# A gated scan and an MLP on one NeuronCore: the planner keeps attention groups open on TensorE

## The chip, the cores and the metric

One core of a Trainium2 chip. The metric is the device time of the whole program in microseconds; the median of three runs is given. The engines are TensorE (PE, matmuls; PEld is its weight loads), VectorE (DVE), ScalarE (ACT), GpSimd (POOL) and SyncE (SP), which here only issues DMAs.

## The reference

```python
# q, k, v, a_re, a_im: (4, 8, 768, 48); per batch and head
mag = sqrt(a_re**2 + a_im**2); scale = minimum(mag, 0.999) / (mag + 1e-6)
for t in range(768):
    S = (a_re + 1j*a_im)[t][:, None] * scale[t][:, None] * S   # S is 48 x 48
    S.real += outer(k[t], v[t])
    y[t] = q[t] @ S.real
x = y as (3072, 384)
h = x @ w_in                                   # 384 -> 2048
g = where(h >= 1, h, where(h <= -1, 0, (h + 1)**2 / 4))
out = g @ w_out                                # 2048 -> 384
```

## The kernel before

**Work.** The 4 x 768 tokens are cut into 12 units of 256 tokens of one batch (two chunks of 128 each). Two units make a block of 512 tokens, six blocks in all. For each unit `gates` (line 569) turns the decays into running products and phases on ScalarE and VectorE, multiplies them into keys and queries, and spreads the rows to heads by ten SBUF-to-SBUF DMAs (`spread`, lines 844 to 881). `attend` (line 898) then does, per chunk, on TensorE: scores `sc` (two PSUM banks of four heads), transposes `tp` of the keys, values `yp` (am times V, plus the old state times the queries) and state products `dp`. VectorE masks scores into `am` (line 997) and adds `dp` to the state `st` (line 974); ScalarE copies `tp` to `kT` (line 939) and `yp` to `xr` (line 1050). Six small DMAs per unit move rows inside `xr` (`move`, line 1062), and `split` (line 1114) makes its high and low parts xH and xL. `moe` (line 1145) runs, for 16 slices f of 128 hidden units, nine matmuls of 512 columns into `h` (line 1160), the activation on ScalarE and VectorE, and nine into the three `o` accumulators (line 1235). All weights are decoded on the chip (`weights`, line 410) during the start and block 0. In blocks below SPARE the activation takes two more ScalarE steps (lines 1195 and 1199) in place of one VectorE step (line 1212). In units below ABS_ACT an absolute value is taken on ScalarE (line 794, shown under its helper's line 608), in later ones on VectorE (line 798).

**Order.** Nothing is issued in program order. Every operation is first recorded in a `Plan` with its engine, a modelled cost, its predecessors and sometimes a due time. `order` (line 169) passes due times back to predecessors, then simulates all engines as a list scheduler: at each step the engine that can start soonest takes, of its ready operations, the one due first. `emit` then issues the instructions in the planned order; each engine works its own list in that order and waits where data are late. SyncE (and VectorE, ScalarE) may hold back for a more urgent operation that will be ready soon (lines 232 to 246, QUEUE and HOLD). DMAs are modelled with a latency, and spreads with LATE_MOVE on top. Before the first MoE product `emit` fills planned gaps of TensorE with idle products (lines 277 to 288 and 1283 to 1290).

**Due times around the change.** DUR (line 312) is the modelled length of a block times SLACK, BEGIN its start. MoE pieces (three matmuls) fall due every DUR/16/6. The attention of a unit of block b is due in a window of block b - 1: WINDOW, EARLY for block 1, HEAD for block 0 (lines 908 to 914), and it is cut into five `visit`s (line 1077) spread evenly over the window. The parts of a visit are glued: when one is planned and the next already has all its predecessors planned, that one is forced next (lines 271 to 273). When not, TensorE may take MoE pieces in between.

**PSUM and SBUF places.** Attention tiles rotate through three PSUM banks `at0` to `at2`, so a part may have to wait until VectorE or ScalarE has emptied the bank that it takes. A batch's state rotates through two buffers (line 955). The upper triangular mask and the ones behind it are one tile, `sums` (line 334).

Of the kernel before, what the change touches and what calls it, by code (L numbers as in the profile page):

```python
# [10 lines left out]
F32 = mybir.dt.float32  # L11
# [53 lines left out]
LATE_MOVE = 1000  # L65
TABLE = 1294
FIRST = 81000
SLACK = 1.04
# [4 lines left out]
QUEUE = (2, 0.0)  # L73
WINDOW = (0.0, 0.7)
EARLY = (0.15, 1.05)
HEAD = ((15000, 8000), (8000, 2000))
HOME = 4
SPARE = 2
# [3 lines left out]
ABS_ACT = 5  # L82
# [42 lines left out]
class Plan:  # L125
# [43 lines left out]
    def order(self):  # L169
# [35 lines left out]
        forced = []  # L205
        while done < n:
# [4 lines left out]
            else:  # L211
                best = None
                for e in free:
                    while avail[e] and avail[e][0][1] in taken:
                        heapq.heappop(avail[e])
# [10 lines left out]
                t, e = best  # L226
                while wait[e] and wait[e][0][0] <= t:
# [44 lines left out]
            if nxt is not None and not left[nxt]:  # L272
                forced.append(nxt)
# [48 lines left out]
def gated_scan_moe(  # L322
# [11 lines left out]
    sums = const.tile([P, 2, P], F32, name="sums")  # L334
    mask = sums[:, 0]
    make_upper_triangular(nc, mask)
    nc.gpsimd.memset(sums[:, 1], 1.0)
# [560 lines left out]
    def attend(u):  # L898
# [25 lines left out]
        def transposes(c):  # L924
            cs = slice(c * CH, (c + 1) * CH)
            out = []
            for g in range(2):
# [19 lines left out]
                carry.setdefault("kT", []).append(KT)  # L947
            return out

        def products(c):  # L950
            kT = carry.pop("kT")
            DP = bank([P, NH, D], f"dp_{u}_{c}")
            V_c = carry["V"]
            old = carry.get(b)
            ST = tl(turn_of(f"st{b % 2}", 2), [HR, NH, D], F32, f"st_{u}_{c}")
            carry[b] = ST

            def run():
                for i in range(NH):
                    for a in (0, 64):  # L960
# [4 lines left out]
                            V_c[0].get()[:, V_c[1], i * D : (i + 1) * D],  # L965
# [4 lines left out]
            def tail():  # L970
                if old is None:
                    fn = lambda: V_.tensor_copy(ST.get(), DP.get()[:HR])
                else:
                    fn = lambda: V_.tensor_tensor(ST.get(), old.get(), DP.get()[:HR], op=ALU.add)
                pl.op("DVE", dve(DM), fn, r=[DP] + ([old] if old else []), w=[ST])

            return [(NH * 124, run, [*kT, V_c[0]], DP, tail)]
# [33 lines left out]
        def values(c, ams, st):  # L1011
# [5 lines left out]
            def part(prs):  # L1017
                Y = bank([P, len(prs), CH], f"yp_{u}_{c}_{prs[0]}")

                def run():  # L1020
                    for i, pr in enumerate(prs):
                        for kind in (0, 1):
                            if kind == 0 and st is None:
                                continue
                            for e in range(2):
# [3 lines left out]
                                if kind == 0:  # L1029
# [4 lines left out]
                                        start=True,  # L1034
                                        stop=False,
                                    )
                                else:
# [4 lines left out]
                                        start=st is None,  # L1042
                                        stop=True,
# [46 lines left out]
        if part == 0:  # L1090
            carry.pop("kT", None)
        state_after = lambda c: part * NC + c < S // CH - 1
        for c in range(NC):
# [9 lines left out]
            pending = (ams, carry.get(b))  # L1103
# [476 lines left out]
```

## Time and profile before

| | us |
|---|---|
| median of 3 runs | 578.7 (578.28 to 579.27) |
| the profiled execution, its own time | 577.35 |
| its span | 575.6 |
| TensorE busy | 561.4 (98%) |
| VectorE busy | 434.5 (75%) |
| ScalarE busy | 406.1 (71%) |
| first MoE product starts at | 70.41 |
| last o product ends near | 568.2 |

The span is the profiler's first to last instruction; the execution's own time holds a little more around it. Matmuls are pipelined, so a single one looks longer than what it adds: nine in mid-stream add 2.04 us. The gap of a group of products is therefore read from start to start.

### The profile page before, as it was taken

What the parts mean: (1) busy time and instruction counts of PE and PEld (TensorE: products, weight loads), DVE (VectorE), ACT (ScalarE), POOL (GpSimd) and SP (SyncE); (2) the same over time, 40 slices, a digit from 0 to 9 for tenths busy, and PEclk for the clock granted to TensorE, in tenths of its full rate; (3) what the DMA queues carried; (4) which work ended last, traced back from release to release, by engine and by line L of the source; (5) the groups of instructions that cost most, each with busy time, mean ns of one, the idle gap of its engine ahead of it and who ended that gap; (6) DMA issues with size and microseconds to landing.
All of it is one profiled execution on the core that took longest, in us unless ns stands there. A gap on an engine that the chain in (4) does not pass through costs nothing.

```text
span 575.6 us, 9984 instructions
## 1 busy us (share of the span) xinstructions
PE 561.4 (98%) x3922; PEld 478.4 (83%) x3922; DVE 434.5 (75%) x625; ACT 406.1 (71%) x654; POOL 1.7 (0%) x20
## 2 busy tenths in 40 slices
PE   8999999999999999999999999999999999999995
PEld 7798978888888888888888888888888888888883
DVE  4999999999979498579589878887885544455452
ACT  7776799887998998975576666667643333369972
POOL 1000000000000000000000000000000000000000
PEclk9999999999999999999999999999999999999999
DMA  8676571773641614712601613402312200078811
GB/s 352 250 198 192 163 262 55 192 282 114 188 173 48 195 68 125 237 57 82 174 2 52 202 56 102 153 2 85 114 56 72 74 1 7 21 265 309 298 42 61
DMA packets 23527, 77.42 MB, mean 134 GB/s; under 512 B 4528, under 2 KB 10288, under 8 KB 23472
## 3 DMA queue, kind: packets, MB, share of 16 engines
q1 hardware_dynamic: 23472, 76.70, 40.8%
q8 instruction: 33, 0.54, 0.4%
q14 instruction: 22, 0.18, 0.1%
HBM read 51.90 MB, written 4.72 MB: 98 GB/s over the span
## 4 chain that ended last, share of the span: by engine, by line
PE 78%; DVE 12%; ACT 5%; DMA 2%; issue 1%; SPq 0%; ACTq 0%; DVEq 0%
PE o L1235 30%; PE h L1160 29%; PE sc L989 6%; PE yp L1038 3%; PE yp L1030 3%; PE dp L962 2%; PE tp L933 1%; PE idle L1290 1%; ACT ai L608 1%; DVE kq L725 1%; DMA xr<-xr 1%; DMA ai<-in_art_dram 1%; DVE g L1204 1%; ACT x L608 1%; DVE raw_i L440 1%
## 5 line engine op out<-in xcount | busy, mean ns | idle before, releaser
L1160 PE MATMUL h<-xH,wi 128*128 128x512 f32 x576 | 180.6, 395 | 1.2 <-DVE g L1204 0.9
L1235 PE MATMUL o<-gh,wo 128*128 128x512 f32 x576 | 180.4, 394 | 0.0
L1160 PEld LDWEIGHTS h<-xH,wi 128*128 128x128 f32 x576 | 106.2, 188 | 22.6 <-DVE g L1204 1.1
L1235 PEld LDWEIGHTS o<-gh,wo 128*128 128x128 f32 x576 | 106.3, 188 | 21.6 <-issue 0.7
L1204 DVE TENSOR_TENSOR g<-h,s 128x512 f32<-128x512 f32 x96 | 65.9, 687 | 63.1 <-ACT s L1185 45.6
L1160 PE MATMUL h<-xL,wi 128*128 128x512 f32 x288 | 112.6, 391 | 0.0
L1235 PE MATMUL o<-gl,wo 128*128 128x512 f32 x288 | 112.5, 391 | 0.0
L1185 ACT ACTIVATE s<-h,cst 128x512 f32<-128x512 f32 x96 | 65.7, 685 | 42.0 <-PE h L1160 38.9
L1218 ACT CAST gh<-g 128x512 fp32r<-128x512 f32 x96 | 59.1, 616 | 46.0 <-DVE g L1212 43.6
L1222 DVE TENSOR_TENSOR gl<-g,gh 128x512 fp32r<-128x512 f32 x96 | 66.0, 687 | 31.9 <-ACT gh L1218 31.8
L1160 PEld LDWEIGHTS h<-xL,wi 128*128 128x128 f32 x288 | 54.1, 188 | 12.1 <-DVE xL L1137 0.4
L1235 PEld LDWEIGHTS o<-gl,wo 128*128 128x128 f32 x288 | 54.1, 188 | 11.6
L608 ACT ACTIVATE ai<-ai 128x768 f32<-128x768 f32 x49 | 41.2, 843 | 19.1 <-DVE ai L777 8.6
L989 PE MATMUL sc<-hd 96*128 96x128 f32 x384 | 49.6, 278 | 0.0
L989 PEld LDWEIGHTS sc<-hd 96*128 96x128 f32 x384 | 47.0, 192 | 2.2
L1212 DVE SCALAR_TENSOR_TENSOR g<-s,g 128x512 f32<-128x512 f32 x64 | 44.2, 691 | 1.8
L1038 PE MATMUL yp<-am,V 128*64 128x128 f32 x384 | 35.5, 273 | 0.2 <-DVE am L997 0.2
L997 DVE TENSOR_TENSOR am<-sc,sums 128x512 f32<-128x512 f32 x48 | 32.5, 683 | 3.1 <-PE sc L989 2.8
L1290 PE MATMUL idle<-sums,ident 128*128 128x128 f32 x238 | 31.3, 291 | 1.7 <-POOL sums masks.py:66 1.7
L1030 PE MATMUL yp<-hd,st 96*64 96x128 f32 x320 | 32.1, 278 | 0.3 <-DVE am L997 0.3
L1290 PEld LDWEIGHTS idle<-sums,ident 128*128 128x128 f32 x238 | 30.3, 206 | 2.5 <-POOL sums masks.py:66 1.7
L402 ACT ACT_TABLE_LOAD x21 | 26.9, 1283 | 0.4
(104 smaller groups left out, 651.6 us busy)
## 6 DMA issues: line engine op xcount, KB each, us to landing
chk<-in_wl_dram SPq DMA_DIRECT2D x16, 768.0 KB, 5.2
kq<-in_kq_dram SPq DMA_DIRECT2D x12, 768.0 KB, 4.7
ai<-in_ari_dram SPq DMA_DIRECT2D x10, 768.0 KB, 6.1
hd<-x SPq DMA_DIRECT2D x24, 288.0 KB, 4.1
hd<-kq SPq DMA_DIRECT2D x24, 288.0 KB, 4.9
raw_i<-in_wl_dram SPq DMA_DIRECT2D x8, 768.0 KB, 4.6
raw_o<-in_wl_dram SPq DMA_DIRECT2D x8, 768.0 KB, 5.8
V<-in_v_dram SPq DMA_DIRECT2D x12, 384.0 KB, 3.2
```

Of the source, the lines that this page charges most:

```text
L608: lambda: A_.activation(out(), src(), f, **kw),
L989: PE_.matmul(SC.get()[:, i, :], t[:, 0, cs], t[:, 1, cs], start=True, stop=True)
L1030: PE_.matmul(o_, st.get().rearrange("p h e -> p (h e)")[:, lo : lo + 64], head(h)[:, 1, cs], start=True, stop=False,)
L1038: PE_.matmul(o_, V.get()[:, c, lo : lo + 64], ams[pr // 2].get()[:, 2 * (pr % 2) + e, :], start=st is None, stop=True,)
L1160: PE_.matmul(H.get(), weight["i", f // 2].get()[:, f % 2, part, sl], x.get()[:, j, :], start=j == 0 and n == 0, stop=j == NJ - 1 and n == 2,)
L1185: lambda: A_.activation(SS.get(), H.get(), AF.Relu, bias=c_half, scale=-0.5 if spare else 0.5),
L1204: lambda: V_.tensor_tensor(G.get(), H.get(), SS.get(), op=ALU.max),
L1212: lambda: V_.scalar_tensor_tensor(G.get(), SS.get(), 1.0, G.get(), op0=ALU.min, op1=ALU.mult),
L1218: pl.op("ACT", act(T), lambda: A_.copy(GH.get(), G.get()), r=[G], w=[GH])
L1222: lambda: V_.tensor_tensor(GL.get(), G.get(), GH.get().bitcast(F32), op=ALU.subtract),
L1235: PE_.matmul(PO[m].get(), weight["o", f // 2].get()[:, f % 2, part, sl], g.get(), start=f == 0 and n == 0, stop=f == NF - 1 and n == 2,)
L1290: PE_.matmul(idle["h1"], ident, mask, start=True, stop=True)
```

## The change

The planner gets a `closed` part: when a part is taken whose glued successor exists, TensorE takes nothing but that successor, and idles until it is ready. The state of a batch is one tile that is added to in place. The old state times the queries comes after am times V in the accumulation. In `moe` the o pieces are recorded one step behind the h pieces instead of LAG steps; their due times keep LAG. `mask` is a tile of its own, and `sums` is built a second time in the place of the second am tile. Eight constants of the planner and of the split of work change.

```diff
@@ -62,24 +62,24 @@
 LOADS = "SP"
 LOAD, MOVE = 410.0, 240.0
 LATE = 2000
-LATE_MOVE = 1000
+LATE_MOVE = 300
 TABLE = 1294
 FIRST = 81000
-SLACK = 1.04
+SLACK = 1.0
 LAG = 3
 SPREADS = 0
 SPREAD = ("SP", "ACT")
 HOLD = {'DVE': (2, 2000.0), 'ACT': (2, 2000.0)}
-QUEUE = (2, 0.0)
-WINDOW = (0.0, 0.7)
-EARLY = (0.15, 1.05)
+QUEUE = (1, 20000.0)
+WINDOW = (0.3, 0.7)
+EARLY = (0.15, 0.9)
 HEAD = ((15000, 8000), (8000, 2000))
 HOME = 4
-SPARE = 2
+SPARE = 1
 LEAD = 8000
 WARM = 0.85
 BRIDGE = 4
-ABS_ACT = 5
+ABS_ACT = 3
 LO_PE = 3
 INFLATE = 1.6
 SPLIT_DUE = 3000
@@ -203,6 +203,7 @@
         done = 0
         taken = set()
         forced = []
+        closed = None
         while done < n:
             if forced:
                 i = forced.pop()
@@ -211,6 +212,16 @@
             else:
                 best = None
                 for e in free:
+                    if e == "PE" and closed is not None:
+                        if closed in taken:
+                            closed = None
+                        elif left[closed]:
+                            continue
+                        else:
+                            t = max(free[e], ready[closed])
+                            if best is None or t < best[0]:
+                                best = (t, e)
+                            continue
                     while avail[e] and avail[e][0][1] in taken:
                         heapq.heappop(avail[e])
                     while wait[e] and wait[e][0][1] in taken:
@@ -224,6 +235,10 @@
                     if best is None or t < best[0]:
                         best = (t, e)
                 t, e = best
+                if e == "PE" and closed is not None:
+                    forced.append(closed)
+                    closed = None
+                    continue
                 while wait[e] and wait[e][0][0] <= t:
                     _, i = heapq.heappop(wait[e])
                     if i not in taken:
@@ -269,8 +284,8 @@
                 if not left[s]:
                     enable(s)
             nxt = self.glued.get(i)
-            if nxt is not None and not left[nxt]:
-                forced.append(nxt)
+            if nxt is not None:
+                closed = nxt
         self.start, self.end, self.due = start, end, due
         return sorted(range(n), key=lambda i: (start[i], i))
 
@@ -331,9 +346,10 @@
 
     ident = const.tile([P, P], F32, name="ident")
     make_identity(nc, ident)
-    sums = const.tile([P, 2, P], F32, name="sums")
-    mask = sums[:, 0]
+    mask = const.tile([P, P], F32, name="mask")
     make_upper_triangular(nc, mask)
+    sums = sb.tile([P, 4, CH], F32, tag="am1", name="sums", bufs=1)[:, :2]
+    make_upper_triangular(nc, sums[:, 0])
     nc.gpsimd.memset(sums[:, 1], 1.0)
     consts = [math.log(1e-6), math.pi / 2, 0.5, TINY, T_MIN, 0.0, 1.0, DECAY]
     cst = const.tile([P, len(consts)], F32, name="cst")
@@ -944,16 +960,16 @@
                     )
 
                 out.append((4 * 83, run, [hd[h // 3] for h in GROUPS[g]], TP, tail))
-                carry.setdefault("kT", []).append(KT)
+                carry.setdefault(("kT", c), []).append(KT)
             return out
 
         def products(c):
-            kT = carry.pop("kT")
+            kT = carry.pop(("kT", c))
             DP = bank([P, NH, D], f"dp_{u}_{c}")
-            V_c = carry["V"]
-            old = carry.get(b)
-            ST = tl(turn_of(f"st{b % 2}", 2), [HR, NH, D], F32, f"st_{u}_{c}")
-            carry[b] = ST
+            first = b not in carry
+            if first:
+                carry[b] = tl(f"st{b % 2}", [HR, NH, D], F32, f"st_{b}")
+            ST = carry[b]
 
             def run():
                 for i in range(NH):
@@ -962,19 +978,19 @@
                         PE_.matmul(
                             DP.get()[a : a + 64, i, :],
                             kT[i // 4].get()[:, k : k + 64],
-                            V_c[0].get()[:, V_c[1], i * D : (i + 1) * D],
+                            V.get()[:, c, i * D : (i + 1) * D],
                             start=True,
                             stop=True,
                         )
 
             def tail():
-                if old is None:
+                if first:
                     fn = lambda: V_.tensor_copy(ST.get(), DP.get()[:HR])
                 else:
-                    fn = lambda: V_.tensor_tensor(ST.get(), old.get(), DP.get()[:HR], op=ALU.add)
-                pl.op("DVE", dve(DM), fn, r=[DP] + ([old] if old else []), w=[ST])
-
-            return [(NH * 124, run, [*kT, V_c[0]], DP, tail)]
+                    fn = lambda: V_.tensor_tensor(ST.get(), ST.get(), DP.get()[:HR], op=ALU.add)
+                pl.op("DVE", dve(DM), fn, r=[DP], w=[ST])
+
+            return [(NH * 124, run, [*kT, V], DP, tail)]
 
         def scores(c):
             cs = slice(c * CH, (c + 1) * CH)
@@ -1019,7 +1035,7 @@
 
                 def run():
                     for i, pr in enumerate(prs):
-                        for kind in (0, 1):
+                        for kind in (1, 0):
                             if kind == 0 and st is None:
                                 continue
                             for e in range(2):
@@ -1031,16 +1047,16 @@
                                         o_,
                                         st.get().rearrange("p h e -> p (h e)")[:, lo : lo + 64],
                                         head(h)[:, 1, cs],
-                                        start=True,
-                                        stop=False,
+                                        start=False,
+                                        stop=True,
                                     )
                                 else:
                                     PE_.matmul(
                                         o_,
                                         V.get()[:, c, lo : lo + 64],
                                         ams[pr // 2].get()[:, 2 * (pr % 2) + e, :],
-                                        start=st is None,
-                                        stop=True,
+                                        start=True,
+                                        stop=st is None,
                                     )
 
                 def tail():
@@ -1087,9 +1103,8 @@
 
         todo_visits = []
         pending = None
-        if part == 0:
-            carry.pop("kT", None)
         state_after = lambda c: part * NC + c < S // CH - 1
+        state_of = lambda: carry.get(b)
         for c in range(NC):
             before = [] if pending is None else values(c - 1, *pending) + products(c - 1)
             sc, ams = scores(c)
@@ -1100,8 +1115,7 @@
             else:
                 visit(sc)
                 visit(tp)
-            pending = (ams, carry.get(b))
-            carry["V"] = (V, c)
+            pending = (ams, state_of())
         last = values(NC - 1, *pending)
         if state_after(NC - 1):
             last = last + products(NC - 1)
@@ -1249,11 +1263,11 @@
                     due=t0 + STEP * (f + LAG - 0.5 + m / 6),
                 )
 
-        for k in range(NF + LAG):
+        for k in range(NF + 1):
             if k < NF:
                 gemm1(k)
-            if k >= LAG:
-                gemm2(k - LAG)
+            if k:
+                gemm2(k - 1)
         for m in range(NJ):
             OB = tl(turn_of("s", 3), [P, T], F32, f"ob_{blk}_{m}")
             i = pl.op(
```

## Rows read from the trace of the kernel before

**Rows 1.** the page's busy times, the whole span
```profile
PE 561.4 (98%) x3922; PEld 478.4 (83%) x3922; DVE 434.5 (75%) x625; ACT 406.1 (71%) x654; POOL 1.7 (0%) x20
```

**Rows 2.** stretch, length, busy us of PE, PEld, DVE, ACT, POOL; PEclk, DMA share, GB/s
```profile
41.16:64.75 23.59, 22.39 (x338) 21.25 (x336) 23.45 (x32) 17.50 (x28) 0.00 (x0) 1.00 0.61 190
64.75:70.41 5.66, 5.40 (x50) 5.21 (x47) 5.20 (x9) 2.98 (x6) 0.00 (x0) 1.00 0.50 146
70.41:153.00 82.59, 81.36 (x609) 68.87 (x610) 81.03 (x114) 73.43 (x115) 0.00 (x0) 1.00 0.58 189
153.00:238.00 85.00, 85.00 (x564) 71.63 (x563) 63.30 (x90) 80.33 (x131) 0.00 (x0) 1.00 0.41 125
```

**Rows 3.** the chain that ended last, in order of time: start, us, what
```profile
33.29 8.04 PE idle L1290 x72
...
65.89 4.04 DMA xr<-xr
...
226.13 2.26 PE o L1235 x9
...
230.43 2.04 PE o L1235 x9
```

**Rows 4.** TensorE's timeline, attention of units 3 and 4: start, us, instruction
```profile
138.93 1.05 PE L989 MATMUL sc<-hd 96*128 96x128 f32 x8
...
141.20 0.82 PE L933 MATMUL tp<-ident,hd 96*128 96x96 f32 x8
...
157.78 0.50 PE L933 MATMUL tp<-ident,hd 96*128 96x96 f32 x4
...
164.29 0.49 PE L933 MATMUL tp<-ident,hd 96*128 96x96 f32 x4
```

**Rows 5.** VectorE's timeline at the same places
```profile
140.14 0.54 DVE L974 TENSOR_TENSOR st<-st,dp 96x384 f32<-96x384 f32 x1
140.60 0.68 DVE L997 TENSOR_TENSOR am<-sc,sums 128x512 f32<-128x512 f32 x1
...
159.71 1.29 DVE L997 TENSOR_TENSOR am<-sc,sums 128x512 f32<-128x512 f32 x2
```

**Rows 6.** SyncE's DMA issues, timeline
```profile
34.55 2.01 SPq L392 DMA_DIRECT2D hd<-kq  x3
...
226.16 4.15 SPq L392 DMA_DIRECT2D hd<-x  x5
230.36 3.47 SPq L392 DMA_DIRECT2D hd<-kq  x5
234.04 3.67 SPq L392 DMA_DIRECT2D xr<-xr  x6
```

**Rows 7.** DMA issues by line: KB each, median us to landing
```profile
hd<-kq SPq DMA_DIRECT2D x24, 288.0 KB, 4.9
```

**Rows 8.** groups of instructions by line and shape: busy us, mean ns, idle before
```profile
L608 ACT ACTIVATE ai<-ai 128x768 f32<-128x768 f32 x49 | 41.2, 843 | 19.1 <-DVE ai L777 8.6 <-DMA ai<-in_ari_dram 4.1 <-DVE ai L622 3.4
L1212 DVE SCALAR_TENSOR_TENSOR g<-s,g 128x512 f32<-128x512 f32 x64 | 44.2, 691 | 1.8
...
L1195 ACT ACTIVATE s<-s,cst 128x512 f32<-128x512 f32 x32 | 23.1, 723 | 0.5
...
L1199 ACT ACTIVATE s<-s 128x512 f32<-128x512 f32 x32 | 20.1, 628 | 0.4
...
L798 DVE TENSOR_SCALAR ai<-ai 128x768 uint32<-128x768 uint32 x7 | 3.9, 556 | 1.5 <-ACT ai L608 1.4
```

**Rows 9.** POOL and ScalarE at the start, timeline
```profile
1.36 0.29 POOL masks.py:66 TENSOR_SCALAR_AFFINE_SELECT sums<-sums 128x128 f32<-128x128 f32 x1
...
4.03 0.93 ACT L608 ACTIVATE x<-ai,cst 128x768 f32<-128x768 f32 x1 [1.68 <-DMA ai<-in_art_dram]
```

**Rows 10.** busy us by stretches, the end of the span
```profile
568.20:572.00 3.80, 0.20 (x3) 0.09 (x2) 0.29 (x2) 0.66 (x2) 0.00 (x0) 1.00 0.68 220
572.00:576.00 4.00, 0.00 (x0) 0.00 (x0) 0.00 (x0) 0.00 (x0) 0.00 (x0) 0.69 0.04 10
```

## The prediction

> **What bounds the kernel now.** I read the page's busy shares first, then the busy time by stretches, then the chain that ended last, then TensorE's timeline around attention. TensorE is busy 98% of the span [rows 1]. By stretches [rows 2] it is full, 85.00 of 85.00 us, once block 1 runs, and 81.36 of 82.59 in block 0; ahead of the first MoE product (70.41 us) it works on the attention of units 0 and 1 (22.39 of 23.59 us) and then fills 5.40 of 5.66 us with idle products while the moves of `xr` land (4.04 us in the chain, [rows 3]). The granted clock is 1.00 throughout, 2.4 GHz. VectorE is nearly full too in block 0 (81.03 of 82.59) but has room in block 1 (63.30 of 85), where ScalarE is the fuller one (80.33). So behind 70.41 us a change gains only by taking work or switches off TensorE, ahead of it by starting the first product earlier; and it loses by any stall of TensorE. A switch has a price: nine o products behind an attention visit take 2.26 us in the chain, nine in mid-stream 2.04 [rows 3], so 0.22 us for each return from a visit.
>
> The profiled execution took 577.35 us (575.6 of span and 1.75 around it); the median of the three runs is 578.7, 1.35 higher. I sum against 577.35 and add 1.35 at the end.
>
> **Open groups.** The planner now picks nothing else for TensorE between two glued parts. Each of units 2 to 11 has five visits (lines 1093 to 1108), 50 in all. In TensorE's timeline I find two that MoE products broke: unit 3's (scores at 138.93, transposes at 141.20) and unit 4's (four transposes at 157.78, the other four at 164.29) [rows 4]. Joining them saves 2 x 0.22 = 0.44 us. If TensorE must wait instead: unit 3's transposes needed the state add (0.54 us from 140.14) and the first am of the next chunk (0.68 us from 140.60), so from the end of the scores at 139.98 to 141.28, with the first transposes fitting in, some 1.2 us; unit 4's second half needed the first of the two am's of 159.71, done near 160.4 [rows 5], while the first half ended at 158.28: 2.1 us. Ends: 0 to 3.3 us. I take 0, because unit 4's first visit now falls due 13 us later against MoE (0.15 x 89.2, below), when VectorE's backlog is gone, and unit 3's place moves as well. What queues behind a waiting TensorE is every MoE product, and so h, then ScalarE's s and VectorE's g.
>
> **Due times.** DUR is SLACK x (66,048 + 23,200 ns): 92.8 us becomes 89.2. For units from block 2 on, WINDOW gave each unit 0.35 x 92.8 = 32.5 us for five visits, one per 6.5 us; now 0.2 x 89.2 = 17.8, one per 3.6 us. A piece of three MoE products is due every STEP/6, 0.97 and now 0.93 us, so 6.7 pieces between two visits become 3.8. Where none is left between two, a switch falls away. Ends: none of the 32 gaps of those units, or 15 (3.3 us); I take three, 0.66 us, since the transposes still wait for am and the next visit for kT, which keeps the gaps apart. The last visit of a block was due 20.4 us before the next block's begin (0.78 of DUR) and is now due 17.0 us before it (0.81). Behind it come the copy, six `xr` moves, xH and xL. Their cover is the rest of the block's MoE: in front of block 1 those steps left TensorE 5.66 us without real work [rows 2], and at the second handover the moves were issued only at 234.04, behind ten `hd` spreads of 226.16 [rows 6]. As unit 6's first visit falls due 13 us later, its spreads now rank behind the moves, so I cost the handover at nothing; without that, 7.6 us of spreads return, and 5.7 + 7.6 = 13.3 is still inside 17.0. EARLY ends sooner (0.9 for 1.05): unit 3's last visit is due at 0.875 of block 0 instead of 0.935, 11 us before block 1 instead of 6, which only helps there.
>
> **LATE_MOVE.** The planner believes that the `hd` spreads land 0.7 us sooner. Ahead of unit 0's scores it puts idle products for 0.85 of the planned gap (line 286): the filler of 8.04 us from 33.29 [rows 3] shrinks by 0.6. The chain goes through the filler, not through a transfer, so the data were there before. When? The three `hd` spreads of kq were issued over 2.01 us from 34.55 [rows 6]; the scores of the first group need the first two, the second of them issued near 35.2, and the large kq spreads take 4.9 us to land [rows 7]: 40.1, against the filler's end at 41.33. So there are about 1.2 us to gain at most, and 0 if the second group's heads wait instead. I take 0.6, and that it reaches the first MoE product, since TensorE is the fuller engine in between.
>
> **QUEUE.** SyncE no longer holds itself free for a more urgent transfer unless that one is 20 us more urgent. At worst one spread's issue (0.6 us, a third of 2.01 [rows 6]) gets in front of the first `xr` move; at best 0.2 us of holding goes. I take 0.
>
> **SPARE, ABS_ACT.** Block 1 loses two ScalarE steps in each of 16 f (723 and 628 ns) and gains one on VectorE (691 ns) [rows 8]: 21.6 us off ScalarE, 11.1 us onto VectorE, which goes from 63.3 to 74.4 of 85 us [rows 2]. Both are hidden under a full TensorE. Units 3 and 4 take the absolute value on VectorE: 2 x 0.56 = 1.1 us more, for 2 x 0.84 less on ScalarE [rows 8]. Both lie in block 0, where VectorE's room is 82.59 - 81.03 = 1.56 us: hidden by that alone, and if the cover is gone up to 1.1 us. I take 0.
>
> **The rest at nothing.** The state in place: the same count of adds, and each already follows the products behind the y products that read the old state. am times V first: the same matmuls, and am and state are both older than the visit. Ends: 0.1 us either way. o products built one step behind: their due times keep LAG, so only ties move. The separate mask adds a memset and a select on POOL (0.29 us, [rows 9]) before the constants that ScalarE first needs at 4.03, when it still waits for a DMA [rows 9]. That `sums` sits in the second am's place makes that am wait for the last running sums, which TensorE has behind it when it turns to filler at 33.29 [rows 3], ahead of any scores.
>
> **Sum.** 577.35 - 0.44 - 0.66 - 0.6 = 575.65; with 1.35 the median is 577.0 us, 0.3% less.
>
> **Rivals.** *Nothing that can be told* (0.31): the open rule acts on two visits of 50, the scores end up waiting for their transfer, no gap closes; 578.7 - 0.44 = 578.3. For it: TensorE is full and its products are the same. Against it: the filler lies in the chain.
> *TensorE stalls in open groups* (0.23): at both places it waits as priced, and nothing else comes: 578.7 + 3.3 = 582.0. For it: VectorE is full up to 153 us, and closer visits leave am and state less time; it decides from the point at which the stalls exceed the 1.7 us gained, about one VectorE queue of three operations. Against it: 48 visits ran unbroken.
> *The clock falls in such a wait* (0.03): with TensorE out of work at the end, the granted clock went from 1.00 in 568.2 to 572 to a mean of 0.69 in the next 4 us [rows 10]. If each stall brought as much work again at 1.2 GHz, the 3.3 us would count twice: 585.3. The Trainium skill (TensorE: Matmul & The Clock Gate, HAM oscillation) says that waits between bursts of products put TensorE back to its lower clock, so that the next burst starts cold; by that rule keeping the engine open is worse than breaking a group. The rows agree for an engine left empty; no row has it for a wait as short as 2 us.
>
> **Numbers.** A difference under 0.2% (1.2 us) a measurement of this kernel can't tell from none. Faster 0.43, same 0.31, slower 0.26. The faster case by itself reaches from 573.7 (all gains at their far ends: 0.44 + 3.3 + 1.2) to 577.5. The range joins the stalls: 573.7 to 582.0.
>
> **What would show it.** Right: no MoE product inside a visit; a filler before unit 0's scores of about 7.4 us and the first h near 69.8; fewer than 50 separate visits; `xr` moves ahead of the next `hd` spreads at a handover; block 1's VectorE at 74 us. Wrong: a wait of TensorE for am or st, in block 0 above all; a first h later than 70.4; a wait of h for xH or xL at a block's start.

## The result, and the profile after

The changed kernel takes 579.99 us (median of 20 runs, 577.99 to 582.48) against 578.71 for the kernel before (20 runs, 577.72 to 580.62): a ratio of 1.0023, 95% interval 1.0012 to 1.0033. It is a little slower, by about as much as can be told from nothing. The time lies inside the forecast range, and on the other side of the old time than the forecast of 577.0. The profiled execution took 577.99 us (span 576.2), the fastest of its 20, so its trace shows the loss at its smallest; `after_again` below has a trace of an ordinary execution. (The diff changes seven constants: LATE_MOVE, SLACK, QUEUE, WINDOW, EARLY, SPARE and ABS_ACT. The section on the change says eight.)

The page's busy times and the busy time by stretches of the changed kernel (columns as in [rows 2]), against [rows 1, 2]:

```profile
PE 560.3 (97%) x3916; PEld 476.9 (83%) x3916; DVE 446.0 (77%) x643; ACT 388.8 (67%) x620; POOL 2.0 (0%) x22
```

```profile
41.16:64.75 23.59, 21.78 (x331) 20.64 (x331) 23.49 (x33) 17.48 (x27) 0.00 (x0) 1.00 0.63 196
...
70.41:153.00 82.59, 81.67 (x613) 69.42 (x613) 80.93 (x114) 70.78 (x109) 0.00 (x0) 1.00 0.53 180
153.00:238.00 85.00, 83.93 (x558) 70.39 (x557) 73.58 (x109) 64.07 (x102) 0.00 (x0) 1.00 0.39 122
```

VectorE's busy time rises by 11.5 us and ScalarE's falls by 17.3, most of it in block 1, as asked. What matters stands in TensorE's column: in block 1 it is no longer full (83.93 of 85.00, before 85.00), and in the attention ahead of block 0 it works 21.78 us where it worked 22.39. TensorE's timeline at the start shows the second place, and the first gain of the forecast with it:

```profile
32.82 7.53 PE L1304 MATMUL idle<-mask,ident 128*128 128x128 f32 x66
40.19 2.02 PE L1005 MATMUL sc<-hd 96*128 96x128 f32 x16
42.04 0.49 PE L949 MATMUL tp<-ident,hd 96*128 96x96 f32 x4
43.97 0.55 PE L949 MATMUL tp<-ident,hd 96*128 96x96 f32 x4 [1.43 <-DVE am L1013]
...
69.89 0.74 PE L1174 MATMUL h<-xH,wi 128*128 128x512 f32 x2
```

The filler is 7.53 us, six products fewer than the 72 of before (8.20 us in this view, 8.04 in the chain of [rows 3]), and the first h comes at 69.89, 0.52 earlier. The second transposes wait 1.43 us for the masked scores, which come when VectorE gets to them; before, it was 0.82. So the 0.67 us that the filler lost is nearly all waited for again here. From the first h to the small product behind the last o (fp, at 568.70, before at 568.21) the loop takes 498.81 us against 497.80. So in this pair of traces 0.5 us are won at the start and 1.0 lost behind it. TensorE's listed waits in the loop are 2.0 us where before had 1.2. One of 0.93 at 77 us stands in both; the new one is at the handover from block 0 to block 1. TensorE's row, and the chain of waits there, in order of time (pieces under 0.2 us left out):

```profile
157.47 0.73 PE L1174 MATMUL h<-xH,wi 128*128 128x512 f32 x2 [1.03 <-DVE g L1218]
```

```profile
148.28 5.13 DMA xr<-xr
153.43 0.41 ACT xH L1144
153.96 0.37 issue
154.33 0.39 ACT xH L1144
154.72 0.63 ACT s L1209
155.48 0.50 issue
156.18 0.53 ACT s L1213
156.73 0.70 DVE g L1218
157.47 0.97 PE h L1174 x3
```

TensorE waits 1.03 us there for g. ScalarE works in order: the activation of a slice (s) stands behind casts to xH that wait for a move of `xr`, and the move, 16 KB, takes 5.13 us to land. ScalarE also has a step on the decays of a later unit (line 624, 0.84 us from 155.25) between the last two steps of s. SyncE's queue at this handover and at the next:

```profile
144.44 2.62 SPq L408 DMA_DIRECT2D hd<-x  x4
147.17 0.52 SPq L408 DMA_DIRECT2D ai<-in_ari_dram  x1
147.73 1.14 SPq L408 DMA_DIRECT2D xr<-xr  x2
...
228.65 1.16 SPq L408 DMA_DIRECT2D hd<-x  x2
229.89 3.91 SPq L408 DMA_DIRECT2D xr<-xr  x6
```

Four spreads and a load go out ahead of the first two moves; at the second handover two spreads do, and the other eight follow the moves, as was forecast. The late moves by themselves don't make the wait: in the kernel before, all ten spreads went first and the moves still later, and TensorE did not wait there. Its queue, and TensorE's scores of unit 4:

```profile
151.18 4.71 SPq L392 DMA_DIRECT2D xr<-xr  x6
```

```profile
155.30 1.95 PE L989 MATMUL sc<-hd 96*128 96x128 f32 x16
```

In the changed kernel TensorE has MoE products alone from 145.26 to 164.41: no attention visit lies in the handover that would give ScalarE time. From the second handover on, s waits for the output's transfers, since it takes a buffer that an `out` transfer still reads. The same row of the list of waits of the whole run, of the kernel before and of the changed one (total, times, longest):

```profile
ACT s L1185 <- DMA out_dram<-ob: 1.5, 3, 0.8
```

```profile
ACT s L1199 <- DMA out_dram<-ob: 7.6, 7, 2.3
```

In this trace none of these seven reaches TensorE.

### The profile page after: what moved, and what is told of

Read it like the earlier page. It is cut to its first block, busy times and chain, and to the rows that moved or that the text cites. A ratio compares the mean times of both kernels' runs of the same rounds, so it can differ in the third digit from the quotient of the medians.

```text
span 576.2 us, 9961 instructions
## 1 busy us (share of the span) xinstructions
PE 560.3 (97%) x3916; PEld 476.9 (83%) x3916; DVE 446.0 (77%) x643; ACT 388.8 (67%) x620; POOL 2.0 (0%) x22
## 4 chain that ended last, share of the span: by engine, by line
PE 83%; DVE 6%; DMA 4%; ACT 4%; issue 1%; SPq 1%; ACTq 0%; DVEq 0%
PE o L1249 33%; PE h L1174 32%; PE sc L1005 7%; PE yp L1054 4%; PE yp L1046 3%; PE dp L978 3%; PE tp L949 2%; DMA xr<-xr 2%; DMA out_dram<-ob 1%; ACT ai L624 1%; DMA ai<-in_art_dram 1%; SPq L408 1%; DVE kq L741 1%; DVE x L850 1%; DVE raw_i L456 0%
## 5 line engine op out<-in xcount | busy, mean ns | idle before, releaser
L1226 DVE SCALAR_TENSOR_TENSOR g<-s,g 128x512 f32<-128x512 f32 x80 | 55.2, 690 | 2.3
L624 ACT ACTIVATE ai<-ai 128x768 f32<-128x768 f32 x47 | 39.4, 842 | 13.3 <-DVE ai L793 5.4
L1013 DVE TENSOR_TENSOR am<-sc,mask 128x512 f32<-128x512 f32 x48 | 32.3, 683 | 5.9 <-PE sc L1005 5.8
L1304 PE MATMUL idle<-mask,ident 128*128 128x128 f32 x232 | 29.9, 287 | 1.7 <-POOL mask masks.py:66 1.7
L1304 PEld LDWEIGHTS idle<-mask,ident 128*128 128x128 f32 x232 | 28.9, 202 | 2.5 <-POOL mask masks.py:66 1.7
L1054 PEld LDWEIGHTS yp<-am,V 128*64 128x64 f32 x384 | 22.5, 136 | 7.9 <-issue 4.3
```

The lines of the kernel that those rows point to most:

```text
L624: lambda: A_.activation(out(), src(), f, **kw),
L1054: PE_.matmul(o_, V.get()[:, c, lo : lo + 64], ams[pr // 2].get()[:, 2 * (pr % 2) + e, :], start=True, stop=st is None,)
L1226: lambda: V_.scalar_tensor_tensor(G.get(), SS.get(), 1.0, G.get(), op0=ALU.min, op1=ALU.mult),
L1304: PE_.matmul(idle["h1"], ident, mask, start=True, stop=True)
```

## The experiments

Each version was run 4 to 20 times; a ratio is to the kernel before on the same chip, with its 95% interval. The record also has the mean granted clock of every execution. A stretch at 1.2 GHz lowers it: the trace of `new_constants` below has one such stretch and a mean of 0.994, that of `three_windows_back` two, the second twice as long, and 0.989, and the two traces of the changed kernel have none from 30 us on and means of 0.996 and 0.995.

**The changed kernel again.** 

> The changed kernel unchanged, for a second trace. Its runs spread from 578.0 to 582.5 us, and the trace in hand is the fastest of them. 'Edge' theory (the constants move unit 4's attention out of the end of block 0, so h waits there for VectorE's g, 1.03 us): ratio to before 1.002, and the second trace shows the same wait near 157 us, longer if the run is longer. 'Lead' theory (LATE_MOVE 300 lets unit 0's scores start 0.6 us earlier, so late spreads now stop TensorE): the second trace, if longer, shows the extra wait between 40 and 66 us.

Measured: 1.0017 (1.0001 to 1.0034). Its trace is 2 us longer than the one above, and the loop takes 500.86 us with 3.3 us of waits. The wait of the start is about the same (1.49), the one of the first handover 1.18, and at the second handover the wait of s reaches TensorE, here and once more (0.49 at 258.00):

```profile
250.90 0.69 ACT L1199 ACTIVATE s<-h,cst 128x512 f32<-128x512 f32 x1 [1.54 <-DMA out_dram<-ob]
```

```profile
252.39 0.73 PE L1174 MATMUL h<-xH,wi 128*128 128x512 f32 x2 [0.75 <-DVE g L1218]
```

**Structure or constants.** `old_constants` leaves open groups, state in place, o pieces and the rest as changed and puts all seven constants back; `new_constants` does the reverse, in the kernel before.

```diff
-LATE_MOVE = 300
-SLACK = 1.0
-QUEUE = (1, 20000.0)
-WINDOW = (0.3, 0.7)
-EARLY = (0.15, 0.9)
-SPARE = 1
-ABS_ACT = 3
+LATE_MOVE = 1000
+SLACK = 1.04
+QUEUE = (2, 0.0)
+WINDOW = (0.0, 0.7)
+EARLY = (0.15, 1.05)
+SPARE = 2
+ABS_ACT = 5
```

> The changed kernel with all seven constants back (LATE_MOVE, SLACK, QUEUE, WINDOW, EARLY, SPARE, ABS_ACT); open groups, state in place, am first and the o order stay. 'Edge' and 'lead' both say: back to before or near it, ratio 1.000, but for one stall in unit 3's open visit of 1.0 to 1.3 us (1.002 at most), and a spread of runs like before's. 'Open' theory (the open groups are what costs): ratio 1.002 to 1.004, as the changed kernel or above it.

> The kernel before with the seven new constants alone; groups may be broken, the state has two buffers, the old state's product comes first. 'Edge' and 'lead': as slow as the changed kernel, ratio 1.002, with the wait of h for g near 157 us of 1.0 us and the first h near 69.9. 'Open': back to 1.000 or under it (0.999 by the 0.5 us earlier start).

Measured: `old_constants` 0.9987 (0.9971 to 1.0003), `new_constants` 1.0022 (1.0003 to 1.0041). The loss comes with the constants: on one chip the changed kernel's median is 580.09 us (`after_again`), with the old constants put back 578.60. The structure costs nothing that can be told, and gains nothing either. With the old constants the open rule does wait, at the place that the forecast named (unit 3) and for the operation it named:

```profile
138.71 1.05 PE L1005 MATMUL sc<-hd 96*128 96x128 f32 x8
140.56 1.15 PE L949 MATMUL tp<-ident,hd 96*128 96x96 f32 x8 [0.79 <-DVE st L990]
```

In `new_constants` the wait at the start does more than last. TensorE's timeline, and the busy time of 1 us stretches behind it (last three columns: granted clock, DMA share, GB/s):

```profile
44.24 0.55 PE L933 MATMUL tp<-ident,hd 96*128 96x96 f32 x4 [1.50 <-DVE am L997]
```

```profile
45.00:46.00 1.00, 1.00 (x7) 0.78 (x6) 1.00 (x3) 0.30 (x1) 0.00 (x0) 0.50 0.83 209
46.00:47.00 1.00, 1.00 (x11) 1.00 (x12) 1.00 (x3) 0.00 (x0) 0.00 (x0) 0.50 0.81 152
47.00:48.00 1.00, 1.00 (x16) 1.00 (x14) 0.96 (x3) 0.02 (x1) 0.00 (x0) 0.50 0.34 76
```

The granted clock is 0.50, 1.2 GHz, for three microseconds behind a wait of 1.50; that is some 1.5 us of work lost, and the first h comes at 71.50. Nine other traces with this wait, 1.36 to 1.50 us long, keep 1.00; the changed kernel's two (1.43 and 1.49) are among them. By the recorded clocks the six slowest-clocked of the twelve executions of `new_constants` (0.991 to 0.994) have a median of 581.69 us and the other six (0.995 to 0.998) 579.65, against 579.43 for the kernel before. So its ratio comes in good part from the clock, and that it equals the changed kernel's does not show that the cause is the same.

**The due windows.** `due_times_only` puts the new WINDOW and SLACK alone into the kernel before, `due_times_spare_1` SPARE = 1 as well:

```diff
-SLACK = 1.04
+SLACK = 1.0
-WINDOW = (0.0, 0.7)
+WINDOW = (0.3, 0.7)
```

> The kernel before with WINDOW (0.3, 0.7) and SLACK 1.0 alone. Its start is that of before (first h near 70.4, first wait of unit 0's transposes 0.8 us). 'Edge' theory (attention moved off the block ends is what costs): waits of h for g of 0.5 to 1.5 us near 160 and near 250, none in before, and a ratio of 1.002 to 1.004. Rival 'start' (the longer wait of unit 0's transposes, 1.43 to 1.50 us for 0.82, behind which one trace shows the clock at 1.2 GHz for 3.2 us, is what costs): 1.000.

> The kernel before with WINDOW and SLACK as changed, and SPARE 1. 'ScalarE in the bare stretches': most of the 1.0% that WINDOW and SLACK cost alone is gone, ratio 1.001 to 1.004, no wait of 2 us near 204. If SPARE is no part of it: 1.008 to 1.010 again.

Measured: 1.0098 (1.0077 to 1.0119) and 1.0058 (1.0032 to 1.0083). The windows moved into the old setting cost a whole per cent, and SPARE = 1 gives part of it back. In the first trace the wait that was expected near 160 is not there, the one near 250 is (1.41 us at 256.61). The longest lies in the middle of block 1, at neither handover: ScalarE waits for a load, with s queued behind it; TensorE runs dry and comes back at half its clock:

```profile
199.53 0.85 ACT L608 ACTIVATE ai<-ai 128x768 f32<-128x768 f32 x1 [2.34 <-DMA ai<-in_ari_dram]
```

```profile
204.86 0.72 PE L1160 MATMUL h<-xH,wi 128*128 128x512 f32 x2 [2.17 <-DVE g L1204]
```

```profile
206.00:208.00 2.00, 2.00 (x6) 1.63 (x5) 1.15 (x2) 2.00 (x5) 0.00 (x0) 0.50 1.02 409
208.00:210.00 2.00, 2.00 (x7) 1.56 (x7) 0.69 (x1) 2.00 (x5) 0.00 (x0) 0.71 0.40 164
```

My theory by now was that the windows lose the time on their own account. `late_window` asked whether a window that ends later (0.85, SLACK 1.02, groups breakable, four s buffers) fills the handover again:

```diff
-SLACK = 1.0
+SLACK = 1.02
-WINDOW = (0.3, 0.7)
+WINDOW = (0.3, 0.85)
-            if nxt is not None:
-                closed = nxt
+            if nxt is not None and not left[nxt]:
+                forced.append(nxt)
```

> A version that may beat both, with attention spread further towards the block ends: the changed kernel with breakable groups, four s buffers, WINDOW (0.3, 0.85) and SLACK 1.02. By 'edge', visits nearer to the handover cover it: no wait of h above 0.3 us behind 165, ratio 0.998 to 1.000. If only visits at the start of a block, as before had them, cover the handover: 1.001 to 1.002.

Measured: 1.0100 (1.0078 to 1.0122). The waits did not go (2.00 us at 168.16, 0.76 at 253.52), and at the third handover an `out` transfer holds VectorE's g back, and TensorE for 3.39 us; the clock is 0.50 in 345 to 347:

```profile
342.37 0.69 DVE L1218 TENSOR_TENSOR g<-h,s 128x512 f32<-128x512 f32 x1 [4.99 <-DMA out_dram<-ob]
```

```profile
343.11 0.73 PE L1174 MATMUL h<-xH,wi 128*128 128x512 f32 x2 [3.39 <-DVE g L1218]
```

`windows_back` is the test of the theory: the changed kernel with WINDOW and SLACK alone as before; `three_windows_back` has the old EARLY too.

```diff
-SLACK = 1.0
+SLACK = 1.04
-WINDOW = (0.3, 0.7)
+WINDOW = (0.0, 0.7)
```

> The changed kernel with WINDOW and SLACK alone back at (0.0, 0.7) and 1.04; the other five constants, the open groups and all the rest stay as changed. Theory A, the due windows are what the change lost by, on their own account: with them back the waits at the handovers of blocks go and the ratio falls below the changed kernel's 1.0023, to 0.997 to 1.000. Theory B, the seven constants only work as a set (each other one put back alone made the changed kernel slower): 1.003 to 1.010, slower than the changed kernel, and its waits lie elsewhere.

> As windows_back, and EARLY back at (0.15, 1.05) too, so that all due times are those of the kernel before; LATE_MOVE, QUEUE, SPARE and ABS_ACT stay as changed. Theory A: 0.997 to 1.000, and block 0 to 1 has its visits at the block's end again, as before. Theory B: 1.003 to 1.010.

Measured: 1.0123 (1.0099 to 1.0147) and 1.0140 (1.0118 to 1.0162). The theory fell: with all due times as before, the kernel is slower than with the new ones. In `windows_back` the open group of unit 3 waits 1.59 us for the state, and the clock falls behind it:

```profile
142.46 1.15 PE L949 MATMUL tp<-ident,hd 96*128 96x96 f32 x8 [1.59 <-DVE st L990]
```

```profile
144.00:146.00 2.00, 2.00 (x6) 1.61 (x5) 2.00 (x2) 0.63 (x2) 0.00 (x0) 0.50 0.00 0
```

In `three_windows_back` TensorE has two long waits. The first h waits for xH until 74.20, since the `xr` moves (issued from 65.98 in `windows_back`, 66.02 here) run beside more spreads and land in 4.6 and 5.9 us (medians) where the changed kernel's took 2.7. And the open group of unit 3 waits for the state, behind VectorE's queue:

```profile
74.20 1.22 PE L1174 MATMUL h<-xH,wi 128*128 128x512 f32 x2 [2.96 <-ACT xH L1144]
```

```profile
146.21 1.54 PE L949 MATMUL tp<-ident,hd 96*128 96x96 f32 x8 [2.65 <-DVE st L990]
```

```profile
143.07 1.76 DVE L850 TENSOR_TENSOR kq<-kq,ai 128x1536 f32<-128x1536 f32 x1
144.74 0.96 DVE L476 TENSOR_TENSOR wi<-raw_i,wi 128x768 fp32r<-128x768 f32 x1
145.61 0.55 DVE L990 TENSOR_TENSOR st<-st,dp 96x384 f32<-96x384 f32 x1
```

```profile
146.00:148.00 2.00, 1.79 (x9) 1.73 (x10) 2.00 (x5) 0.69 (x2) 0.00 (x0) 0.50 0.80 295
148.00:150.00 2.00, 2.00 (x6) 1.58 (x5) 2.00 (x3) 0.27 (x1) 0.00 (x0) 0.50 1.03 418
150.00:152.00 2.00, 2.00 (x6) 1.52 (x6) 1.23 (x3) 0.32 (x1) 0.00 (x0) 0.50 0.14 58
```

A kq product and the decoding of weights (wi) lie ahead of the state add in VectorE's list; the group that may not be broken stands still for 2.65 us, and six microseconds at 1.2 GHz follow. That is the rival of stalls in open groups and the clock's rival together, at the predicted place, in a setting in which the change does not run.

The clock is a part of what the slow mixtures lose. All executions of `late_window` (0.988 to 0.993), `windows_back` (0.991 to 0.993) and `three_windows_back` (0.989 to 0.991) have a lower mean than any of the kernel before beside them (0.995 to 0.998). An estimate from these means, with TensorE taken as full: a mean lower by 0.001 costs about 0.58 us. That gives 3.5 of the 6.2 us that `late_window` lost, 2.5 of 7.3 for `windows_back`, 3.9 of 8.4 for `three_windows_back` and 1.8 of 5.0 for `due_times_only`.

**The other constants**, each put back alone into the changed kernel: LATE_MOVE 1000, SPARE 2, QUEUE (2, 0.0), ABS_ACT 5.

```diff
-LATE_MOVE = 300
+LATE_MOVE = 1000
```

> The changed kernel with LATE_MOVE back at 1000 alone. 'Lead': the runs get their narrow spread back and the ratio falls to 1.000; the first h is at 70.4 again. 'Edge': the wait at the end of block 0 stays at 0.5 to 1.5 us, the start is 0.5 us later, ratio 1.002 to 1.004.

```diff
-SPARE = 1
+SPARE = 2
```

> The changed kernel with SPARE back at 2 alone (block 1's activation takes 21.6 us more of ScalarE and 11.1 us less of VectorE). Theory 'ScalarE in the bare stretches' (with attention drawn together, block 1 has 20 us of MoE alone, where three steps of ScalarE per f leave no room for a late load): slower than the changed kernel, ratio 1.003 to 1.006, with a wait of h for g near 200. If SPARE is a step that costs nothing, as the prediction has it: 1.002.

```diff
-QUEUE = (1, 20000.0)
+QUEUE = (2, 0.0)
```

> The changed kernel with QUEUE back at (2, 0.0) alone, so that SyncE holds back for more urgent transfers again. If QUEUE is part of the cost (at the first handover the spreads of unit 4 and a load went out before the moves of xr): the wait of h near 157 shrinks and the ratio falls to 1.000 or 1.001. If it costs nothing, as predicted: 1.002, the wait of 1.0 us stays.

```diff
-ABS_ACT = 3
+ABS_ACT = 5
```

> The changed kernel with ABS_ACT back at 5 alone: units 3 and 4 take the absolute value on ScalarE, 1.1 us off VectorE in block 0, 1.7 us onto ScalarE. If VectorE's 1.1 us is what starves h at the end of block 0: the wait near 157 goes, ratio 1.000 to 1.001. If it is hidden, as predicted: 1.002, the wait stays at about 1 us.

Measured: 1.0028 (1.0012 to 1.0044), 1.0039 (1.0020 to 1.0059), 1.0052 (1.0033 to 1.0072) and 1.0098 (1.0073 to 1.0122). None is below the changed kernel's 1.0023, and ABS_ACT's is clear of its interval; LATE_MOVE's can't be told from it. The wait of h at the first handover is in all four traces (0.65 to 1.52 us, between 158 and 169 us), and the one that was expected near 200 for SPARE in none. So none of the four is shown to be the one that loses; the planner makes another order from each mixture, and no mixture of constants tried is shown to beat either whole set. In the trace of `queue_old` the first h comes at 71.26, 1.4 us later than in the changed kernel's, since it waits 1.23 for xH. In that of `abs_5` the loop takes 500.90 us with 2.7 of waits; its trace is the fastest of its six executions (580.71), and three of the others have clocks of 0.991 to 0.993, so a part of its loss is the clock's. Where the rest goes stays open.

**The start.** `early_scores` gives the kernel before three pairs of idle products fewer ahead of unit 0's scores, LATE_MOVE's effect on the filler alone. `fill_wait` gives the changed kernel six pairs of idle products where the transposes wait.

```diff
+                if u == 0:
+                    extra[len(pl.ops)] = -3
                 visit(sc)
...
+        if i in extra:
+            n += extra[i]
```

```diff
                 visit(tp)
+                if u == 0:
+                    extra[visits[-1][1]] = 6
...
+        if i in extra:
+            n = max(n, 0) + extra[i]
```

> The kernel before with three pairs of idle products (0.67 us) fewer ahead of unit 0's scores; nothing else moves in the plan. The scores start 0.6 us earlier, while am, in VectorE's queue, comes when it came: the wait of unit 0's second transposes grows from 0.82 to about 1.45 us, as in the changed kernel. If 'start' is a cost of its own (the clock falls behind that wait in some executions, 1.6 us each): ratio 1.001 to 1.002 and single runs 1.5 us above the rest. If it costs nothing by itself: 0.999 to 1.000, and all of the changed kernel's loss lies behind the first h.

> The changed kernel with six pairs of idle products (1.34 us) ahead of the second transposes of unit 0, in the wait for am of 1.43 to 1.50 us. 'Start' theory (in some executions that wait drops the clock to 1.2 GHz for about 3 us, 1.6 us each time): the wait shrinks to 0.1 to 0.2 us, no drop, a narrower spread with nothing above 582, ratio 1.000 to 1.001. 'Edge': the same ratio as the changed kernel, 1.002.

Measured: 1.0017 (1.0002 to 1.0033) and 1.0002 (0.9988 to 1.0017). In `early_scores` the scores come 0.6 us sooner, the second transposes wait 1.42 us for am, and the lead is gone at the first h (70.81, before 70.41), which waits for the `xr` moves:

```profile
70.35 0.86 ACT L1133 CAST xH<-xr 128x256 fp32r<-128x256 f32 x2 [2.11 <-DMA xr<-xr]
```

```profile
70.81 0.73 PE L1163 MATMUL h<-xH,wi 128*128 128x512 f32 x2 [0.93 <-ACT xH L1133]
```

Both results lie where the theory 'start' put them, and `fill_wait`'s interval leaves out the 1.002 of 'edge', though its trace keeps both handover waits (0.99 us at 157.60, 0.73 at 252.77). By the clocks, six of the twelve executions of `early_scores` are at 0.993 (median 579.90; the other six 579.28), and none of `fill_wait` is under 0.996 (median 579.16). So in the old setting a part of the cost can be the clock's, though no trace shows where it fell in those six. In the changed kernel it is not: 18 of its 20 executions are at 0.995 or above, and their median is that of all 20. Why `fill_wait` is no slower than the kernel before is therefore open; `fill_wait` is 0.2% below the changed kernel's 1.0023, from another set of runs, and the intervals overlap.

`early_scores` shows one thing more. Its plan behind the first h is that of the kernel before and its listed waits there are as short (1.15 us), yet its loop takes 499.41 us, 1.6 longer. So a difference of 1 us in the loop between single traces can't be put down to the listed waits alone.

**The output's buffers.** `four_s` gives s, g and ob four places instead of three in the changed kernel (three lines, one of them shown); `four_s_fill` adds the idle pairs; `old_constants_s4` takes the old constants, breakable groups and four places; `old_constants_s4_fill` adds three idle pairs to that.

```diff
-            SS = tl(turn_of("s", 3), [P, T], F32, f"s_{blk}_{f}")
+            SS = tl(turn_of("s", 4), [P, T], F32, f"s_{blk}_{f}")
```

> The changed kernel with four buffers for s, g and ob instead of three, in the SBUF that the state's second buffers left. 'Edge' theory, its part at the second handover (s waits for the out transfer that still reads ob in its place, so h waits for g, 1.24 us in three of four traces of the new constants): those waits near 252 and 258 go, the median falls by about 1 us, ratio 1.000; the wait near 157 stays. 'Start': no change, 1.002.

> The changed kernel with both repairs: four s buffers and the six filler pairs in unit 0's wait. If the costs are two separate ones ('start' 0.0015 by fill_wait, 'edge' at the second handover 0.0006 by four_s, of the changed kernel's 1.002), the ratio is 0.9995 to 1.000, a little under either repair alone. If both repaired the same thing, 1.000 to 1.001.

> A version that may beat both: the constants and the breakable groups of before, the changed kernel's state in place, am first and o order, and four buffers for s. 'Edge' says that before has no wait at the block ends to lose, except ScalarE's and VectorE's for the out transfers: ratio 0.998 to 1.000. 'Start' says 1.000.

> A version that should beat both: the constants and breakable groups of before, state in place, four s buffers, and three filler pairs (0.67 us) in unit 0's wait of 0.82 us. 'Start' and 'edge' together: ratio 0.997 to 0.999, the runs close together (none above 579.7); by 'edge' alone as old_constants_s4, 0.9986.

Measured: 1.0011 (0.9995 to 1.0026), 1.0013 (0.9995 to 1.0030), 0.9986 (0.9971 to 1.0001) and 0.9993 (0.9979 to 1.0008). None can be told from the kernel before, and the two repairs don't add up. In the trace of `four_s` the waits near 252 and 258 are gone, as expected, and those of the first handover add up to 1.3 us. No version here is shown to beat both kernels.

## Why the prediction missed the sign

**Open groups: the stalls right, the gain not there.** I took 0 of 0 to 3.3 us for stalls, because later due times move the two places; the loop of the changed kernel has no wait for st or am. That is in part luck: with the same windows, `late_1000` waits 0.53 us for the state at unit 3 and `four_s_fill` 0.33. With old due times put back, in whole or in part, it waits 0.79 us (`old_constants`, I had 1.2 for that place), 1.59 (`windows_back`) and 2.65 (`three_windows_back`), inside the 3.3 for both places. The 0.44 us of saved switches did not come. From start to start, three products behind such a part take 0.78 us for 0.68 in mid-stream, so a return costs 0.10 at these places and not 0.22; in TensorE's two timelines unit 3's scores and transposes with their returns take 1.61 us broken and 1.59 joined, unit 4's 2.53 broken and 2.77 joined.

**Due times: the step that failed.** I took 0.66 us for closed gaps and cost the handover at nothing, because the steps behind the last visit fit in the 17 us before the next block. In place of nothing, the two traces of the changed kernel show new waits of h for g at the handovers: 1.03 us, and 1.18 + 0.75 + 0.49. The time was enough, but time was not what ran short. The old window had visits in the handover itself (scores at 239.79, transposes at 248.43 in the trace before; 249.08 and 252.95 in the one after). Without them TensorE takes MoE slices one after another, each of which needs s, g and gh from in-order engines whose next operation waits for a transfer. I had put a price on xH and xL, and none on s behind a landing `xr` move or behind an `out` transfer. Measured: waits in the loop of 2.0 to 3.3 us against 1.2, and a loop of 498.81 to 500.86 against 497.80. That the constants carry the loss is shown (`old_constants`). That it goes through these waits is not: the trace of `old_constants`, which is no slower than before, has 2.03 us of waits and a loop of 498.88 too, and `fill_wait` keeps the handover waits. That WINDOW and SLACK alone are to blame was my theory and fell with `windows_back`. So the handover's term was wrong at 0, and how much of the 1.28 us between the medians it carries stays open. Few gaps closed: 49 separate attention groups lie behind the first h, before 52. I had counted on five fewer, two by the joins and three by closed gaps; of the three that went, two are the joins, so one gap closed (unit 4's scores and transposes).

**LATE_MOVE: right at its place, wrong at the end.** The filler was forecast at about 7.4 us and is 7.53, the first h at 69.8 and is at 69.89. The second number is luck. The longer wait for am took the filler's gain back, so that the second transposes come 0.30 us earlier than before, and TensorE was already 0.31 us ahead when the filler began (32.82 for 33.13); the rest is `xr` moves that landed sooner. By itself (`early_scores`) the 0.6 us turned into a wait for am, and the first h came later (70.81); in `four_s`, with the same start as the changed kernel, it is at 70.67. I had bounded it by the landing of the spreads at TensorE's side and not asked what VectorE does next.

**QUEUE, SPARE, ABS_ACT: the cover held, the sum's form did not.** Block 1's VectorE was forecast at 74.4 us and is 73.58; most spreads follow the `xr` moves at the second handover; no engine became the bound. At the first handover my bound for QUEUE, one spread's issue of 0.6 us ahead of the moves, was too small: four spreads and a load, 3.1 us of issues, went first. And I costed each constant against the old plan, at 0. Put back singly these three make the ratio 0.0016 to 0.0075 larger; and WINDOW and SLACK cost 0.98% when they enter the old setting and 1.00% when they leave the new one (1.0123 less 1.0023). A sum over parts does not hold in a schedule that is planned anew for each mixture.

**The clock's rival** was given 0.03 for the open groups. The traces have it at three kinds of wait: 1.50 us ahead of transposes, 2.17 and 3.39 ahead of h, 1.59 and 2.65 in an open group, each followed by three to some six microseconds at 1.2 GHz. The Trainium skill (TensorE: Matmul & The Clock Gate, HAM oscillation) says that a wait between bursts of products makes the next burst start cold; these traces agree at those places, and not at the nine waits of 1.36 to 1.50 us that kept the clock. The row for a wait as short as 2 us that the prediction lacked is there now. It is not the cause of the changed kernel's slower median: the clock holds in its two traces, and of its 20 executions only two (0.994 and 0.993) have a mean as low as that of a trace with such a stretch.

**The spread.** I added the old distance of 1.35 us between the profiled execution and the median. For the changed kernel it is 2.0 (577.99 to 579.99), in `after_again` 0.1 (579.96 to 580.09): which execution is profiled is chance, and the distance is no property of a kernel to be added to a sum.

**The signs.** Of what the prediction named for being right, the unbroken visits, the filler, the first h, the fewer groups and block 1's VectorE came out, and the order of the moves in part; of what it named for being wrong, none showed in the loop, though at the start the wait for am grew from 0.82 to 1.43 us. The time went the other way all the same: no sign looked at a wait of h for g.

## What to carry to other kernels

Before a stage handover is cost at nothing, ask what independent work the fullest engine has there while its neighbours wait for transfers; look in the trace at what each in-order queue holds *behind* an operation that waits for a DMA, not only at the operation. Here the constants of a planner were worth what their set was worth: test the whole set, the reverse set, and then single ones from both sides before one of them is blamed. The mean clock of every execution can tell what one profile can't: whether a stretch at the lower clock is the rule or the exception. And an engine that may not be given other work while it waits should wait only for operations that are first in their own engine's list.

## What the runs showed of the hardware

TensorE's granted clock fell to 0.50 behind waits as short as 1.50 us (`new_constants`), and stayed at 1.00 behind equal ones in other kernels; behind the wait of the first h it held after 2.30 us in `windows_back` and was 0.50 to 0.52 from 74 to 77 us after 2.96 in `three_windows_back`. The same wait can have two prices. Six moves of 16 KB between SBUF places took a median of 2.7 us to land ahead of the changed kernel's first h, 3.2 in the kernel before, and 4.6 and 5.9 in `windows_back` and `three_windows_back`, where more transfers were under way: 64 to 74 us moved 1.69, 1.80, 2.14 and 2.16 MB.
